# Pooling folds of one batch placed one to a half step, and VectorE's job number and first tile kept in two registers

## The chip, the cores and the metric

The kernel runs on one core of one Trainium2 chip. The metric is the device time of one execution in microseconds (us). Before the change it is 602.16 us, the median of three executions (602.12 to 604.27). The engines are called as the profile calls them: PE is TensorE's matmul, PEld its weight load, DVE is VectorE, ACT is ScalarE, POOL is GpSimd, SP is SyncE, which here only issues transfers.

## The reference, cut to what matters

Attention over pooled keys and values, followed by a mixture of eight experts in which each token goes to one expert:

```python
B, H, S, D = 8, 8, 576, 64                      # q, k, v: (8, 8, 576, 64)
k_p = k.reshape(B, H, 72, 8, D).mean(axis=3)    # every 8 rows of k and of v become one
v_p = v.reshape(B, H, 72, 8, D).mean(axis=3)
scores = q @ k_p.T / sqrt(D)
attn = softmax(scores)                          # over 72 keys
x = (attn @ v_p) -> rows of B*S = 4608 tokens, H*D = 512 wide
logits = x @ w_gate                             # 8 experts, 1024 hidden
e_idx = argmax(logits, axis=1)
out[mask_e] = gate_w * eom * (relu(x[mask_e] @ w1[e]) @ w2[e])
```

## The kernel before, in words

The 4608 tokens are 36 tiles of 128. The program has two parts.

**The attention part** goes through the tiles in half steps: tile i, heads 0 to 3 is half step i, tile i, heads 4 to 7 is half step i.5; there are 72. Each half step does three things for three different tiles, which makes a pipeline. It multiplies queries by pooled keys for its own tile (`scores`, PE, line 276, into one of three PSUM buffers `p_h`); DVE takes the maximum of each row (`peak`, line 282, tile name `m`), and ACT the exponentials (line 288). It transposes the probabilities of the tile two steps back (PE line 300, ACT line 301). And it multiplies those of the tile three steps back by the pooled values (`values`, PE line 310, into `p_y`, one PSUM buffer for each half of the heads); DVE then takes the reciprocals of the sums (line 327, `grec`) and writes the normalised rows out of PSUM (`normalise`, line 333, `xg`). Until line 333 of a half step is done, PE can't start `values` of the half step one whole step later, since both use the same `p_y` buffer.

The order of instructions on each engine is the order in which this loop calls them: every engine is a queue, and nothing is moved later. Work that belongs to no single tile is put between in two ways. `at(step, ...)` puts a call at the end of a certain half step: `at(s, ...)` runs at the end of half step s + 0.5. And `queue` holds generators, each a chain of small pieces of DVE work; `work(n)` (called three times in a half step, with 2, 1 and 1) takes up to n pieces of them. A generator that yields 0 may be taken again at once; one that yields 1 is passed over until the next half step.

The values of a batch b are first needed in the half step that I call f: f is 4.5, 9, 13.5, 18, 22.5, 27 and 31.5 for batches 1 to 7 (batch 0 has code of its own). Their eight rows per key lie side by side in one SBUF buffer, `rows`, loaded by one transfer (line 189). They are summed in three foldings. The first is POOL's (`halve_v`, line 224, five adds of about 0.7 us; three of them called at the end of half step f - 2.5, two at the end of f - 2). The other two are DVE's, for two parts of the buffer, which makes four adds, all of line 228, and called folds 1 to 4 here: fold 1 is `rows` 128x384, fold 2 `vp` 128x192, fold 3 `rows` 128x256, fold 4 `vp` 128x128. They come from the generator `pooled`. Fold 1 needs POOL's first three adds, fold 3 the last two. At the end of half step f PE transposes the folded values (`turn_v`, line 248, tile `vtr`), and ACT copies them for the gates' matmuls. The transfer of the next batch's values (line 189, on SP) goes into the same buffer and so waits for fold 4; the transfers of queries and keys behind it on SP's queue wait with it.

The other generators in `queue` are the routing (`route`): after each four tiles, some twenty pieces of DVE work decide to which expert each token goes, and POOL scatters the tokens' rows (line 441). `pooled` is put ahead of them.

**The expert part** runs the tokens through the experts in jobs of up to three tiles, with loops whose counts are read from a table that the routing made. PE's first layer is line 1031, the second line 1012. On DVE the function `body` (line 1210) is built once for each expert and each job size: it scales the last output of the job before (`last_output`, lines 1206 and 1204), subtracts high parts of the hidden layer (line 1215), splits weights (line 1192) and prepares the next job's inputs (`next_low`, line 1242; the wait is line 1163). Each wait compares a semaphore with a number made of `job` (the number of the job) and `u` (its first tile). Both are expressions: the sum of the counts of all experts before, plus the loop's own counter. At each use the sequencer works the whole sum out anew, in instructions that the trace calls FUSED_REGOPS and the order ISA.

Of the kernel before, what the change touches and what calls it, by code (L numbers as in the profile page):

```python
# [91 lines left out]
def attention_and_routing(ctx, tc, sh, qT, kT, v, wg, wst, xs):  # L92
    nc = tc.nc
# [132 lines left out]
    def pool_v(b, a, n):  # L226
        to = vt[:, part_v(a), 0:n] if n > D else pooled_rows(b)[:, part_v(a)]
        nc.vector.tensor_tensor(to, vt[:, part_v(a), 0:n], vt[:, part_v(a), n:2 * n], op=ALU.add)
# [293 lines left out]
    plan, queue = {}, []  # L522

    def at(step, f, *args):
        plan.setdefault(step, []).append((f, args))

    def pooled(b):
        for a in range(2):
            for n in (2 * D, D):
                pool_v(b, a, n)  # L530
                yield 0

    tick = [0]

# [14 lines left out]
    for b in range(1, B):  # L549
        f = S * b // P + 0.5 * (b % 2)  # L550
        at(f - 8.5, load_k, b)
        at(max(f - 5, 0), load_v, b)
        at(f - 4.5, load_q, b)
        for i, part in enumerate([(w, c, c + 1) for c in range(4) for w in (4, 2)] + [(1, 0, 4)]):
            step = f - 5.5 + 0.5 * (i // 2)
            at(step if step != -0.5 else 0, pool_k, b, nc.gpsimd, *part)
        at(max(f - 2.5, 1.5), scale_k, b)
        at(f - 3, halve_v, b, 0)
        at(f - 2.5, halve_v, b, 1)
        at(f - 2, lambda b: queue.insert(0, [pooled(b), 0, -1]), b)  # L560
        for c in range(3):
            at(f - 0.5 + 0.5 * c, place_v, b, c)
        at(f - 0.5, turn_v, b)
        at(f + 1.5, gate_v, b)
# [163 lines left out]
def experts(st, nc, sh, wst, xs, out):  # L728
# [49 lines left out]
    def mark(eng, hint, which):  # L778
        r, spot = which
        hint[spot] = eng.mark_branch_hint_location(hint[r])  # L780
# [64 lines left out]
    def started(e, size, rows, nth):  # L845
        return rows[E + 1] - 2 - nth if e == 0 and size == 3 else None
# [314 lines left out]
    def _(eng):  # L1161
        def xl(u, k):
            eng.wait_ge(q["xh"], u + k + 1)
            nc.vector.tensor_tensor(xt[:, 1, :, P * k:P * k + P], turned[k], xt[:, 0, :, P * k:P * k + P].bitcast(F32),
                                    op=ALU.subtract).then_inc(q["xl"], 1)
# [5 lines left out]
        def turns(job, read=None, more=None):  # L1171
            if read is not None:
                eng.wait_ge(q["xl"], read)
            eng.wait_ge(q["xd"], LANDED * (job + 1))
            turn(0)
            turn(1)
            if more is None or isinstance(more, int):
                if more:
                    eng.wait_ge(q["xl"], read + 1)
                turn(2)  # L1180
            else:
                with eng.If(more > 0):
                    eng.wait_ge(q["xl"], read + 1)
                    turn(2)
                with eng.Else():
                    turn(2)

        def split(some):
            for e, j in some:
                m, s, hi, lo = piece(e, j)  # L1190
                eng.wait_ge(q["wh"], 8 * e + j + 1 - EARLY)
                nc.vector.tensor_tensor(lo, s, hi.bitcast(F32), op=ALU.subtract).then_inc(q["wl"], 1)
# [10 lines left out]
        def output(k):  # L1203
            nc.vector.tensor_scalar(yb[k], p_y[k], sc[:, k:k + 1], None, op0=ALU.mult).then_inc(q["y"], 1)  # L1204

        def last_output(u):
            eng.wait_ge(q["l2"], u + 1)  # L1207
            output(2)

        def body(e, size, job, u, single, nth, more, last, late, hint):  # L1210
            n = size * P

            def low(f, src, n):
                eng.wait_ge(q["hh"], 8 * job + f + 1)
                nc.vector.scalar_tensor_tensor(ht[:, 1, f, 0:n], src, 0.0, ht[:, 0, f, 0:n].bitcast(F32),  # L1215
                                               op0=ALU.max, op1=ALU.subtract).then_inc(q["hl"], 1)

            def hidden(some, turned=False):
                for f in range(8):
                    low(f, p_h[f % DEEP][:, 0:n], n)  # L1220
                    split(some[f:f + 1])
                    if turned and f == 3:
                        turns(job + 1, u + 2, 3)
                eng.nop().then_inc(q["ad"], 8)

            def hidden_one(some):
                for f in range(9):
                    if f < 8:
                        eng.wait_ge(q["l1"], 8 * job + f + 1)
                        nc.vector.tensor_reduce(sums[:, f], p_h[f % DEEP][:, 0:2 * P].rearrange("p (x n) -> p n x", x=2),  # L1230
                                                axis=AX.X, op=ALU.add).then_inc(q["ad"], 1)
                    if f:
                        low(f - 1, sums[:, f - 1], P)
                        if f - 1 in POS:
                            split(some[POS.index(f - 1):][:1])

            with eng.If(job > 0):  # L1237
                last_output(u)
            done = started(e, size, rows, nth)

            def next_low():
                xl(u + size, 0)
                xl(u + size, 1)
                with eng.If(more > 0):
                    xl(u + size, 2)

            def begin_split(some):
                next_low()
                split(some[2:])

            if done is None:
                choose(eng, e, size, single, nth, hidden, hidden_one, split, done, late)
                next_low()
            else:
                choose(eng, e, size, single, nth, lambda some: (hidden(some), next_low()), None, begin_split, done, late,
                       lambda some: (hidden(some, True), next_low()))
            rest(eng, e, size, single, nth, split, 0, 99, done, late)
            finish(eng, e, size, single, last, split, 0, 4)
            if size == 3:
                mark(eng, hint, PAIRS)  # L1260
            elif e + 1 < E:
                mark(eng, hint, TRIPS)

            def close():
                turns(job + 2, u + size + 2, more)
                y(u, 0, job)
                if size == 3:
                    y(u, 1, job)

            if done is None:  # L1270
                close()
            else:
                with eng.If(done > 0):
                    y(u, 0, job, True)
                    y(u, 1, job, True)
                    with eng.If(counts(rows[0])[0] <= 1):
                        turns(job + 2, u + size + 2, more)
                with eng.Else():
                    close()
# [174 lines left out]
```

## Time and profile before

| | |
|---|---|
| median of three executions | 602.16 us |
| the profiled execution, its own time | 602.74 us |
| its span from first to last instruction | 600.8 us |
| TensorE's granted clock, mean share | 0.999 |
| PE busy | 572.1 us, 95% |
| PEld busy | 518.9 us, 86% |
| DVE busy | 363.7 us, 61% |
| ACT busy | 256.4 us, 43% |
| POOL busy | 223.9 us, 37% |

The 600.8 us are one execution; a busy time is the union of an engine's instructions. The attention part lies between about 9 and 154 us, the expert part between about 153 and 600 us. In nearly every fortieth of the span PE is busy for nine tenths or more, so what counts is where it is not, and on whom it waits there.

### The profile page before, as it was taken

To read this page: it belongs to the slowest core of one execution; us is meant where nothing else is said; L and a number is where in the kernel's file an instruction comes from. 1 tells how busy PE (TensorE), PEld (TensorE's weight loads), DVE (VectorE), ACT (ScalarE), POOL (GpSimd) and SP (SyncE) were. 2 spreads that over 40 slices of the span, in tenths; PEclk is the share of its full clock that TensorE was granted. 3 is DMA by queue.
4 is the path that set the end of the run, shared out by engine and by line. 5 is a ranking of instruction groups with operands and counts; after the bars stand their busy time and mean duration, and the time that the engine had idled before them with its cause. 6 is when DMAs were issued, how large, how long until landed. Compare 5 with 4: busy or idle time off the path is not lost.

```text
span 600.8 us, 11852 instructions
## 1 busy us (share of the span) xinstructions
PE 572.1 (95%) x3427; PEld 518.9 (86%) x3428; DVE 363.7 (61%) x892; ACT 256.4 (43%) x709; POOL 223.9 (37%) x331
## 2 busy tenths in 40 slices
PE   2899999999999999999999999999999999999996
PEld 2798898888888989898989898898998898989895
DVE  6788899988978725698575324664253832232323
ACT  2888988788525304266344121441140430202120
POOL 2849789851526322224224131232202422213131
PEclk9999999999999999999999999999999999999999
DMA  9767888975557433589656213363033112010111
GB/s 338 292 239 289 351 304 314 373 292 163 189 203 193 164 101 116 146 238 327 207 192 202 62 38 88 124 211 64 37 133 99 48 31 69 17 52 19 35 36 35
DMA packets 44683, 96.60 MB, mean 161 GB/s; under 512 B 5515, under 2 KB 28475, under 8 KB 41664
## 3 DMA queue, kind: packets, MB, share of 16 engines
q1 hardware_dynamic: 29328, 48.95, 25.4%
q10 hardware_dynamic: 7488, 27.27, 13.6%
q0 software_dynamic: 7792, 19.61, 9.2%
q14 instruction: 56, 0.46, 0.2%
q8 instruction: 19, 0.31, 0.2%
HBM read 76.36 MB, written 22.91 MB: 165 GB/s over the span
## 4 chain that ended last, share of the span: by engine, by line
PE 68%; issue 2%; DVEq 0%; DVE 0%; POOL 0%; POOLq 0%
PE p_h L1031 34%; PE p_y L1012 33%; PE p_y L665 1%; POOL out L1353 0%; DVE rows L1204 0%; DVEq L1207 0%; PE p_y L1068 0%; DVE q_even L1230 0%; DVEq L793 0%; POOLq L1318 0%; DVEq L767 0%; DVEq L1237 0%; DVEq L926 0%; DVEq L853 0%; DVEq L785 0%
## 5 line engine op out<-in xcount | busy, mean ns | idle before, releaser
L1113 ACT ACTIVATE ht<-p_h 128x384 fp32r<-128x384 f32 (+1 forms) x104 | 46.8, 450 | 246.4 <-PE p_h L1031 219.1
L1353 POOL DMA_INDIRECT out<-rows,dst x41 | 42.2, 1030 | 210.4 <-DVE rows L1204 207.3
L1031 PE MATMUL p_h<-xt,w1b 128*128 128x384 f32 (+1 forms) x736 | 115.5, 317 | 2.0 <-issue 2.0
L1031 PEld LDWEIGHTS p_h<-xt,w1b 128*128 128x128 f32 x736 | 114.4, 189 | 3.3 <-issue 2.9
L1215 DVE SCALAR_TENSOR_TENSOR ht<-p_h,ht 128x384 fp32r<-128x384 f32 (+1 forms) x104 | 52.3, 504 | 100.0 <-ACT ht L1113 90.6
L1012 PE MATMUL p_y<-w2b,ht 128*128 128x512 f32 x480 | 110.4, 390 | 0.0
L1012 PEld LDWEIGHTS p_y<-w2b,ht 128*128 128x128 f32 x480 | 89.8, 188 | 18.4
L1031 PEld LDWEIGHTS p_h<-xt,w1a 128*128 128x128 f32 x640 | 92.7, 190 | 2.6 <-DVE q_even L1230 1.2
L1031 PE MATMUL p_h<-xt,w1a 128*128 128x256 f32 (+1 forms) x640 | 93.7, 306 | 1.2 <-DVE q_even L1230 1.0
L1012 PE MATMUL p_y<-w2a,ht 128*128 128x512 f32 x408 | 94.0, 390 | 0.0
L1012 PEld LDWEIGHTS p_y<-w2a,ht 128*128 128x128 f32 x408 | 76.3, 188 | 15.6
L1204 DVE TENSOR_SCALAR rows<-p_y,sc 128x512 f32<-128x512 f32 x41 | 30.1, 742 | 84.3 <-PE p_y L1012 75.9
L288 ACT ACTIVATE p<-p_h,m 128x72 f32<-128x72 f32 x288 | 69.8, 347 | 16.3 <-DVE m L282 14.3
L310 PE MATMUL p_y<-vbd,pT 128*128 128x162 f32 (+3 forms) x400 | 68.7, 320 | 6.1 <-DVE xg L333 4.4
L1328 POOL DMA_INDIRECT rows<-xs,src x51 | 57.6, 1129 | 25.0 <-POOL src L1324 13.5
L310 PEld LDWEIGHTS p_y<-vbd,pT 128*128 128x128 f32 (+1 forms) x400 | 54.2, 179 | 11.1 <-issue 5.7
L441 POOL DMA_INDIRECT xs<-xg,where x36 | 36.0, 1000 | 38.4 <-DVE grec L327 17.2
L202 POOL TENSOR_TENSOR kq<-kq 128x288 f32<-128x288 f32 (+1 forms) x63 | 42.2, 675 | 17.4 <-DMA kq<-kT 14.4
L276 PE MATMUL p_h<-kbd,q_even 128*128 128x144 f32 (+1 forms) x160 | 28.7, 307 | 11.5 <-DMA q_even<-qT 8.8
L333 DVE TENSOR_TENSOR xg<-p_y,grec 128x240 f32<-128x240 f32 x72 | 35.2, 489 | 1.4
L276 PEld LDWEIGHTS p_h<-kbd,q_even 128*128 128x128 f32 (+1 forms) x160 | 22.8, 191 | 13.6 <-issue 9.5
L1168 DVE STREAM_TRANSPOSE turned<-rows 128x512 f32<-128x512 f32 x51 | 32.4, 686 | 3.2 <-DMA rows<-xs 1.5
(170 smaller groups left out, 657.7 us busy)
## 6 DMA issues: line engine op xcount, KB each, us to landing
stage<-wst ACTq DMA_DIRECT2D x52, 512.0 KB
rows<-v SPq DMA_DIRECT2D x8, 1280.0 KB
kq<-kT SPq DMA_DIRECT2D x7, 1152.0 KB
rows<-xs SPq DMA_DIRECT2D x36, 192.0 KB
stage<-wst SPq DMA_DIRECT2D x12, 512.0 KB, 5.0
kq<-qT SPq DMA_DIRECT2D x4, 1152.0 KB
q_even<-qT SPq DMA_DIRECT2D x3, 1152.0 KB, 8.5
rows<-xs SPq DMA_DIRECT2D x20, 128.0 KB
```

Of the source, the lines that this page charges most:

```text
L202: eng.tensor_tensor(k[:, :, 0:w], k[:, :, 0:w], k[:, :, w:2 * w], op=ALU.add)
L276: nc.tensor.matmul(s[r0:r0 + n, 144 * c:144 * c + 144], q_t[b][:, 2 * a + c, s0:s0 + n], kbd[b % 2][:, 2 * a + c, :], start=True, stop=True)
L288: nc.scalar.activation(pt[i % 3][:, o:o + KEYS], sv[:, h], AF.Exp, bias=m[:, h:h + 1])
L310: nc.tensor.matmul(av[r0:r0 + n, COLS * h:COLS * (h + n_heads)], pT[:, c, r0:r0 + n], vbd[b % 2][:, slot:slot + n_heads].rearrange("p h f ...
L333: nc.vector.tensor_tensor(xg[g][:, j, 0:LEAD + DM].rearrange("p (f h) -> p f h", h=H)[:, :, hs], avv[:, :, 0:GATE + D].rearrange("p h f -> ...
L441: ins = nc.gpsimd.indirect_dma_start(out=whole_rows(xs), out_offset=bass.IndirectOffsetOnAxis(ap=where, axis=0), in_=x.bitcast(I32), in_of ...
L1012: i = mm(to, ht[:, h, f, P * k:P * k + P], w[:, part, o:o + DM], start=(f == 0 and part == 0 and h == 0), stop=(f == 7 and h == 1))
L1031: i = mm(to, w[:, part, o:o + P], x, start=(d == 0 and k == 0), stop=(d == 3 and k == len(terms) - 1))
L1113: act(ht[:, 0, f, 0:size * P], p_h[f % DEEP][:, 0:size * P], AF.Relu).then_inc(q["hh"], 1)
L1215: nc.vector.scalar_tensor_tensor(ht[:, 1, f, 0:n], src, 0.0, ht[:, 0, f, 0:n].bitcast(F32), op0=ALU.max, op1=ALU.subtract).then_inc(q["hl" ...
L1328: nc.gpsimd.indirect_dma_start(out=xm[:, k].bitcast(I32), out_offset=None, in_=xs, in_offset=bass.IndirectOffsetOnAxis(ap=src[:, k:k + 1], ...
L1353: nc.gpsimd.indirect_dma_start(out=out, out_offset=bass.IndirectOffsetOnAxis(ap=dst[:, k:k + 1], axis=0), in_=yb[2 if k == size - 1 else k ...
```

## The change

The generator of the folds yields 1 and not 0, so that a half step takes one fold of a batch, and it is put into the queue half a step earlier. In DVE's part of the expert code two registers are set at the head of each job, and the rest of the job uses these.

```diff
@@ pooled(b)
             for n in (2 * D, D):
                 pool_v(b, a, n)
-                yield 0
+                yield 1
@@ for b in range(1, B)
-        at(f - 2, lambda b: queue.insert(0, [pooled(b), 0, -1]), b)
+        at(f - 2.5, lambda b: queue.insert(0, [pooled(b), 0, -1]), b)
@@ DVE's part of the experts
+        kept = [eng.alloc_register(name) for name in ("job_now", "u_now")]
+
         def body(e, size, job, u, single, nth, more, last, late, hint):
             n = size * P
+            for r, value in zip(kept, (job, u)):
+                eng.reg_mov(r, value)
+            job, u = (nc.s_assert_within(eng.snap(r), 0, most, skip_runtime_bounds_check_because="there are at most 50 slots")
+                      for r, most in zip(kept, (49, 49)))
```

The first place is DVE in half steps 3 to 4.5, where batch 1 is folded (f is 4.5). `m_0_` and `m_1_` are the maxima of two successive half steps, `grec` and `xg` the reciprocals and normalised rows of one half step, `vp_310` the folded values. Before:

```order
L282 TENSOR_REDUCE m_0_287<-p_h 128x4
L327 RECIPROCAL grec_293<-p_y 128x3
L333 TENSOR_TENSOR xg_291<-p_y,grec_293 128x80x3
L282 TENSOR_REDUCE m_1_307<-p_h 128x4
L228 TENSOR_TENSOR rows<-rows 128x3x128
L228 TENSOR_TENSOR vp_310<-rows 128x192
L327 RECIPROCAL grec_293<-p_y 128x5
L228 TENSOR_TENSOR rows<-rows 128x2x128
L333 TENSOR_TENSOR xg_291<-p_y,grec_293 128x80x5
L228 TENSOR_TENSOR vp_310<-rows 128x128
```

After, for the same half steps and two more:

```order
L282 TENSOR_REDUCE m_0_287<-p_h 128x4
L228 TENSOR_TENSOR rows<-rows 128x3x128
L327 RECIPROCAL grec_294<-p_y 128x3
L333 TENSOR_TENSOR xg_292<-p_y,grec_294 128x80x3
L282 TENSOR_REDUCE m_1_308<-p_h 128x4
L228 TENSOR_TENSOR vp_310<-rows 128x192
L327 RECIPROCAL grec_294<-p_y 128x5
L333 TENSOR_TENSOR xg_292<-p_y,grec_294 128x80x5
L282 TENSOR_REDUCE m_0_331<-p_h 128x4
L228 TENSOR_TENSOR rows<-rows 128x2x128
...
L282 TENSOR_REDUCE m_1_353<-p_h 128x4
L228 TENSOR_TENSOR vp_310<-rows 128x128
```

A reciprocal and a normalisation stand where rows are left out. Fold 1 has moved from half step 3.5 to 3, ahead of a normalisation; fold 2 stays in 3.5; fold 3 comes in 4 and fold 4 in 4.5, half a step and a whole step later than before. All batches move alike: folds 1 to 4 stand in half steps f - 1.5, f - 1, f - 0.5 and f, where all four stood in f - 1.

The second place is PE at the end of half step 4.5. Its order around the transposes of the folded values is the same before and after (names of buffers aside); this is after:

```order
L300 MATMUL ptr_1_348<-ident,p_75 128x128 x3
L310 MATMUL p_y<-vbd_69,pT_282 128x162
L310 MATMUL p_y<-vbd_69,pT_282 128x243
L310 MATMUL p_y<-vbd_69,pT_282 128x162
L248 MATMUL vtr_367<-ident,vp_310 128x128 x2
L248 MATMUL vtr_367<-ident,vp_310 64x128
L276 MATMUL p_h<-kbd_72,kq 128x144 x2
```

Nothing moved here: the transposes read what fold 4 writes, and fold 4 now stands in the same half step on DVE.

The third place is DVE at the head of a job in the code of a late expert. Before:

```order
L1237 ISA
L1237 COMPARE_AND_BRANCH
L1207 ISA x4
L1204 TENSOR_SCALAR rows<-p_y,sc 128x512
```

After:

```order
L1215 ISA x4
L1243 COMPARE_AND_BRANCH
L1207 REGISTER_ALU
L1204 TENSOR_SCALAR rows<-p_y,sc 128x512
```

The sums stand once ahead of the branch, and the wait is made from a register by one instruction. (Line numbers behind the change are six higher.) The same happens at `next_low` and at the end of the job. The routing's pieces shift by a few places between the folds, and with them POOL's scatters by one or two places; the instructions themselves are the same.

## Rows read from the trace of the kernel before

**Rows 1.** Stretches: us; busy PE, PEld, DVE, ACT, POOL; clock, DMA, GB/s.
```profile
20.00:154.00 134.00, 126.60 (x972) 113.52 (x973) 116.84 (x422) 113.44 (x448) 94.04 (x130) 1.00 0.78 289
200.00:596.00 396.00, 392.71 (x2177) 356.90 (x2176) 192.45 (x301) 114.24 (x200) 98.55 (x142) 1.00 0.35 104
```

**Rows 2.** Waits of PE: total us, times, longest us.
```profile
PE p_y L310 <- DVE xg L333: 4.4, 6, 1.5
PE p_h L1031 <- DVE q_even L1230: 1.0, 1, 1.0
```

**Rows 3.** Waits of DVE: the folds behind POOL's adds.
```profile
DVE rows L228 <- POOL rows L224: 4.4, 4, 1.6
```

**Rows 4.** Waits of SP's queue: the next batch's values.
```profile
SPq L189 <- DVE vp L228: 72.2, 6, 16.4
```

**Rows 5.** Timeline of DVE, batch 1: start us, us, instruction, [idle before].
```profile
23.83 1.07 DVE L228 TENSOR_TENSOR rows<-rows 128x384 f32<-128x384 f32 x1 [1.60 <-POOL rows L224]
...
26.52 0.61 DVE L228 TENSOR_TENSOR vp<-rows 128x128 f32<-128x128 f32 x1
27.05 0.45 DVE L282 TENSOR_REDUCE m<-p_h 128x4 f32<-128x288 f32 x1
27.42 0.16 DVE L327 RECIPROCAL grec<-p_y 128x3 f32<-128x3 f32 x1
27.62 0.41 DVE L333 TENSOR_TENSOR xg<-p_y,grec 128x240 f32<-128x240 f32 x1
27.94 0.45 DVE L282 TENSOR_REDUCE m<-p_h 128x4 f32<-128x288 f32 x1
...
28.52 0.58 DVE L333 TENSOR_TENSOR xg<-p_y,grec 128x400 f32<-128x400 f32 x1
```

**Rows 6.** Timeline of PE, batch 1.
```profile
23.81 0.72 PE L310 MATMUL p_y<-vbd,pT 128*128 128x162 f32 x4
...
26.75 1.20 PE L310 MATMUL p_y<-vbd,pT 128*128 128x162 f32 x6 [1.10 <-DVE xg L333]
27.79 0.49 PE L248 MATMUL vtr<-ident,vp 128*128 128x128 f32 x3
```

**Rows 7.** Timeline of POOL, batch 1.
```profile
21.71 3.78 POOL L224 TENSOR_TENSOR rows<-rows 128x256 f32<-128x256 f32 x5
...
26.19 5.32 POOL L202 TENSOR_TENSOR kq<-kq 128x288 f32<-128x288 f32 x8 [0.56 <-DMA kq<-kT]
```

**Rows 8.** Timeline of DVE, batch 2.
```profile
40.64 0.54 DVE L228 TENSOR_TENSOR rows<-rows 128x384 f32<-128x384 f32 x1
41.21 0.36 DVE L228 TENSOR_TENSOR vp<-rows 128x192 f32<-128x192 f32 x1
...
42.78 0.18 DVE L379 TENSOR_REDUCE gden<-ex 128x4 f32<-128x32 f32 x1
42.87 0.18 DVE L383 TENSOR_TENSOR pos<-rk,running 128x32 f32<-128x32 f32 x1
...
43.96 0.45 DVE L282 TENSOR_REDUCE m<-p_h 128x4 f32<-128x288 f32 x1
```

**Rows 9.** Timeline of PE, batch 2.
```profile
43.40 0.49 PE L248 MATMUL vtr<-ident,vp 128*128 128x128 f32 x3
```

**Rows 10.** Timeline of DVE, batch 3.
```profile
56.72 1.07 DVE L228 TENSOR_TENSOR rows<-rows 128x384 f32<-128x384 f32 x1 [1.07 <-POOL rows L224]
...
58.69 0.90 DVE L228 TENSOR_TENSOR rows<-rows 128x256 f32<-128x256 f32 x1
```

**Rows 11.** Timeline of PE, batches 3 and 5.
```profile
60.14 1.23 PE L310 MATMUL p_y<-vbd,pT 128*128 128x162 f32 x6 [1.49 <-DVE xg L333]
61.21 0.49 PE L248 MATMUL vtr<-ident,vp 128*128 128x128 f32 x3
...
93.94 1.20 PE L310 MATMUL p_y<-vbd,pT 128*128 128x162 f32 x6 [0.98 <-DVE xg L333]
```

**Rows 12.** The chain that ended last, in order of time: start us, us, what.
```profile
461.72 0.22 DVEq L1207
```

## The prediction

> **What bounds the kernel now.** I read the stretches first, then the waits of PE, then the timelines of the engines that PE waits for. Between 20 and 154 us, the attention part, PE is busy for 126.60 of 134.00 us, and DVE, ACT and POOL work beside it for 116.84, 113.44 and 94.04 us; in the expert part PE is busy for 392.71 of 396.00 us, DVE for 192.45 [rows 1]. So PE sets the end throughout. The change touches no instruction of PE; it can take away only what PE waits for DVE, and add to it. Two such waits count: in six places `values` waits for a normalisation, 4.4 us together, and once, in the expert part, PE waits 1.0 us for a reduction of DVE [rows 2]. If both went, the time would fall by 5.4 us. This is the most that the change can win.
>
> The timelines say where the 4.4 us come from. In batches 1, 3 and 5 DVE does the four folds in one half step, `xg` of that half step is late, and PE stands 1.10, 1.49 and 0.98 us [rows 6, 11]: 3.57 of the 4.4. But why is DVE late there? Fold 1 starts when POOL's third add ends: in batch 1 it had waited 1.60 us, in batch 3 1.07 [rows 5, 10], in four places together 4.4 us [rows 3]. It is POOL that holds up the odd batches, and the length of the folds comes on top.
>
> **The folds, batch by batch.** I take what a DVE instruction costs from start to start in batch 1: `m` 0.37 us (27.05 to 27.42), `grec` 0.20, a normalisation of three heads 0.32 [rows 5]; one of five heads lasts 0.58 where the other lasts 0.41, so I count 0.49. Folds beside an idle POOL: 0.54 and 0.36 for folds 1 and 2 [rows 8], and by size 0.36 and 0.24 for folds 3 and 4. Beside POOL's adds they took 1.07 (fold 1), 0.90 (fold 3) and 0.61 (fold 4) [rows 5, 10].
>
> Batch 1. POOL's five adds run from 21.71 us for 3.78 us [rows 7], and nothing in the change brings them forward, so fold 1 starts at 23.83 as before, only that DVE now stands in front of it with one normalisation and one `m` still undone. From there to the end of fold 4: fold 1, `grec`, `xg` 1.07 + 0.20 + 0.32; `m`, fold 2, `grec`, `xg` 0.37 + 0.36 + 0.20 + 0.49; `m`, fold 3, `grec`, `xg` 0.37 + 0.36 + 0.20 + 0.32; `m`, fold 4 0.37 + 0.24; together 4.87 us, so 28.7 us. The transposes of `vp` stand on PE at 27.79 [rows 6] and read what fold 4 writes: today it ends at 27.13 (26.52 + 0.61), then about 28.7. With folds 3 and 4 at their long durations it is 0.54 + 0.37 more, 29.6. PE thus comes to its next scores 1.0 to 1.9 us later than now. The first of its stalls is already inside this: `values` that started at 23.81 waits until the delayed `xg`, about 25.6, and the 1.10 us at 26.75 go. POOL adds keys from 26.19 us for 5.32 us [rows 7], beside all three later folds, so I take 1.5 us, nearer to the long durations.
>
> Batch 2 waits for no POOL today. Its `m` of half step 9 starts at 43.96, while the transposes start at 43.40 [rows 8, 9]: DVE is behind PE. If nothing in front of this `m` went, fold 4 would end at 43.96 + 0.37 + 0.24 = 44.57, 1.2 us late. But by the order seven small pieces of the routing, 0.09 us from start to start (42.78 to 42.87, rows 8), and fold 4 itself move behind it: 0.63 + 0.24 us less, so 43.7. I take 0.3 us.
>
> Batch 3 has the same sum from fold 1 at 56.72 [rows 10], with nine routing pieces between: 4.87 + 9 x 0.09 = 5.68, so 62.4 us, and 62.9 with the long fold 3, against transposes at 61.21 [rows 11]: 1.2 to 1.7 later. POOL's chain before these adds does not shift by all of what PE has lost by then, which gives some back: 1.2 us.
>
> Batches 4 to 7. Batch 5 is an odd one of the same kind with the smallest stall today (0.98); POOL's lead over the shifted PE has grown, and I take 0.4. Batch 4 I take like batch 2, 0.4. In batches 6 and 7 fold 1 need not wait, and DVE reaches the later half steps less behind, so the new wait and the small stalls that go about cancel: 0.1 and 0. Sum of the folds: 1.5 + 0.3 + 1.2 + 0.4 + 0.4 + 0.1 + 0 = 3.9 us.
>
> The ends of this term: below, the 4.4 us all go and no wait takes their place. Above, no batch gets anything earlier: 1.2 us (batch 2 undiminished) in seven batches, and in the three odd ones `grec`, `xg` and `m` (0.89 us) behind the fold as well: 8.4 + 2.7 = 11.1 us.
>
> Other sides of the move. SP's queue stands 72.2 us in six waits for fold 4 before it may load the next batch's values [rows 4]; fold 4 comes two half steps later, some 2 us, and the queries and keys behind it on that queue too. The next user, POOL, needs these values about three tiles later; I count nothing, and 2 us once if batch 2's came too late. Behind fold 1, which now waits longer in DVE's queue, stand one `grec` and `xg` (PE's `values` wait for it) and `m` (ACT's exponentials): that is in the sums. The waits between dependent folds (0.03 us after the end, as from 41.18 to 41.21, rows 8, where others overlap) go, but their gain is under 0.1 us each.
>
> A rule speaks against spreading the folds. The row: fold 1 took 0.54 us alone and 1.07 beside POOL's adds [rows 5, 8]. The Trainium skill (SBUF — State Buffer, section Who interferes with whom) says that a VectorE instruction with two inputs in SBUF contends with a GpSimd instruction that reads SBUF, and that whichever starts first holds the shared port for its whole length; the trace agrees with the doubling. By the short durations alone the sum of the folds would be 3.4 us, by this rule for every late fold it is the last rival below.
>
> **The registers.** In a late job the sequencer works out `u` in four pieces of about 0.22 us ahead of the last output [rows 12]. After the change it does the same pieces at the head of the job, then compares once; what is saved there is the piece that made `job`. At the later uses one register instruction replaces the sums, some 0.8 us a job, but DVE has 192.45 us of work in 396.00 [rows 1] and PE does not wait for it there. The price lies between -1.0 us (the one wait of PE that DVE causes goes) and +1.0 (it doubles, if the longer head comes at a bad place); I take -0.2.
>
> Sum: 3.9 - 0.2 = +3.7 us. The profiled execution took 602.74 us, which gives 606.4; it was 0.58 us above the median, 602.16, so 605.9 us for the median.
>
> **The rivals.**
> - The new waits and those that go cancel: 602.2 us. For it: PE has DVE behind it by only a little in the even batches, and DVE works off its backlog while PE stands. Against: the sums of batches 1 and 3 are 2.7 us by themselves.
> - The smoothing works: the six waits of 4.4 us go, 597.8 us. For it: DVE's four folds in one half step do make `xg` late. It needs POOL's adds to be done when DVE comes to fold 1 half a step earlier, and fold 4 to end before PE ends `values` of the same half step. Against: in three batches POOL is not even ready for today's place [rows 3], and today's `m` in batch 2 already starts behind the transposes.
> - The folds collide with POOL: folds 2, 3 and 4 in batches 1, 3 and 5 each take 0.5 us more (0.90 against 0.36 to 0.40): 9 x 0.5 = 4.5 on top, 610.4 us. It decides if POOL is at its adds in each of these half steps; with 94.04 of 134.00 us busy it is in most, but scatters are among them. The skill's rule on the shared port would give this.
>
> **How the numbers follow.** The forecast 0.52, with a range of its own from 603.2 to 609; cancelling 0.25; smoothing 0.13; collision 0.10. The measurement tells no change from one of about 0.5%, 3.0 us: below 599.2 is faster, above 605.2 slower. The forecast lies above 605.2 in some three of five cases (0.32), with the collision 0.42 for slower; the rest of the forecast and nearly all of cancelling make 0.43 for the same; smoothing and what is left 0.15 for faster. The range from 599.5 to 609.5 us holds the forecast and cancelling, and leaves out most of smoothing and half of the collision, under 0.2; the ends of the terms, 596.7 (-5.4) and 614.3 (+11.1 + 1.0), lie outside it as all of them would have to fall together.
>
> **What would show it.** Right: PE gets a new wait in its table, `vtr` (line 248) for `vp` (line 228), 3 to 6 us in four to seven places; DVE's wait for POOL's adds grows from 4.4 to 7 us or more; `values` of half step 4 waits in batch 1 in place of that of 4.5; the attention part ends some 4 us later and the expert part is as long as before within 0.5 us; fused register pieces at the wait of `next_low` are nearly gone. Wrong: no wait at `vtr` and no `xg` wait left (smoothing), or `vtr` waits that are matched by waits of `values` that vanished (cancelling), or an expert part that changes by over 1 us, which I hold for moved code and not for the registers.

## The result, and the profile after

| | before | after |
|---|---|---|
| first timing, median of 5 runs, us | 602.17 (602.12 to 604.27) | 610.24 (608.98 to 611.51) |
| ratio, 95% interval | | 1.0123 [1.0098, 1.0147] |
| second timing, ratio | | 1.0086 [1.0070, 1.0102] |
| profiled execution, us; its span | 602.74; 600.8 | 610.24; 608.5 |

The change makes the kernel slower, by 8.1 us in the first timing and 5.2 in the second; 3.7 were forecast, and the range ended at 609.5. The direction and the place of the new wait were right, the size was not. The ratios, here and below, leave out one execution in another state, 2016.15 us, of the kernel called "all four, later".

The waits of PE after, over the whole span: total us, times, longest. Below them the one row of before that is needed beside [rows 2].

```profile
PE vtr L248 <- DVE vp L228: 5.7, 5, 2.0
PE p_y L310 <- DVE xg L333: 1.9, 2, 1.1
PE p_y L665 <- PEq L1425: 1.8, 1, 1.8
PE p_h L1031 <- DVE q_even L1236: 1.0, 1, 1.0
PE p_y L665 <- issue: 0.6, 1, 0.6
```

```profile
PE p_y L665 <- PEq L1419: 1.0, 1, 1.0
```

Against [rows 2]: the six waits for `xg` fell from 4.4 to 1.9 us, and the transposes of `vp` now wait 5.7 us in five places for fold 4, which they did not do at all before; 3 to 6 us in four to seven places were forecast. The wait for `q_even`, the one that the registers could have touched, is 1.0 as it was. Two rows stand after the attention part, where the forecast had nothing: the entry into the expert blocks (line 665 released by the sequencer at line 1425, 1419 before), 1.8 us and 1.0 before, and a new wait of 0.6 us just ahead of it.

The wait of DVE for POOL's adds after, to set against 4.4 in four times [rows 3], and that of SP's queue for fold 4. Before, the seventh of these waits is put down to `rows` and not to `vp` (last line), so 72.2 [rows 4] and 8.8, 81.0 us in seven, stand against 91.8 in seven:

```profile
DVE rows L228 <- POOL rows L224: 5.0, 3, 2.6
```

```profile
SPq L189 <- DVE vp L228: 91.8, 7, 17.3
```

```profile
SPq L189 <- DVE rows L228: 8.8, 1, 8.8
```

The same stretches as in [rows 1]: us, busy PE, PEld, DVE, ACT, POOL, granted clock, DMA share, GB/s.

```profile
20.00:154.00 134.00, 124.57 (x959) 112.54 (x959) 111.92 (x406) 113.99 (x446) 89.44 (x125) 0.99 0.75 278
200.00:596.00 396.00, 393.26 (x2191) 359.08 (x2191) 197.68 (x308) 118.54 (x207) 102.21 (x144) 1.00 0.37 110
```

DVE and POOL are busy for less in the first stretch too, with fewer instructions, and ACT for 0.55 us more with two fewer. PE's clock reads 0.99. The stretches in which it fell, and the first of them in before:

```profile
80.00:83.75 3.75, 1.72 (x15) 1.45 (x14) 3.14 (x6) 2.91 (x13) 3.18 (x5) 1.00 0.50 172
83.75:87.20 3.45, 3.45 (x15) 3.30 (x14) 1.68 (x5) 2.20 (x8) 3.15 (x5) 0.51 0.97 332
180.00:182.70 2.70, 0.87 (x5) 0.59 (x4) 0.56 (x1) 0.00 (x0) 0.25 (x2) 1.00 0.00 0
182.70:186.20 3.50, 3.50 (x10) 2.71 (x9) 3.09 (x5) 2.00 (x2) 2.32 (x3) 0.51 0.89 313
```

```profile
83.75:87.20 3.45, 3.45 (x29) 3.12 (x29) 3.42 (x17) 3.45 (x16) 3.11 (x6) 1.00 1.00 415
```

Twice PE stood still, and in the 3.41 us behind it was granted 1.2 GHz in place of 2.4; the first time it did 15 matmuls, where the kernel before does 29 between the same two times. Half of 3.41 us is 1.7, and PE's lag behind before grows by 1.67 us in the first and 1.54 in the second. Before has none ahead of its last microseconds.

The first fall comes behind the worst of the new waits, in batch 4. DVE, POOL and PE there (start us, us, instruction, [idle before]):

```profile
79.47 0.42 DVE L228 TENSOR_TENSOR rows<-rows 128x256 f32<-128x256 f32 x1
...
80.51 0.45 DVE L282 TENSOR_REDUCE m<-p_h 128x4 f32<-128x288 f32 x1
80.87 1.50 DVE L228 TENSOR_TENSOR vp<-rows 128x128 f32<-128x128 f32 x1
```

```profile
80.43 0.96 POOL L441 DMA_INDIRECT xs<-xg,where  x1 [0.30 <-issue]
81.42 1.36 POOL L202 TENSOR_TENSOR kq<-kq 128x288 f32<-128x288 f32 x2
```

```profile
80.13 0.27 PE L248 MATMUL vtr<-ident,vp 128*128 128x128 f32 x1
82.43 0.44 PE L248 MATMUL vtr<-ident,vp 128*128 128x128 f32 x2 [2.03 <-DVE vp L228]
```

Fold 4, which I had put at 0.24 us, took 1.50 beside POOL's scatter and adds of keys, and all of it lies within PE's wait of 2.03. All folds of `vp` (2 and 4) after 20 us, after and before (min/median/max ns):

```profile
L228 DVE TENSOR_TENSOR vp<-rows x14: 281/349/1500, 25.9 to 135.7; 128x192 f32<-128x192 f32 x7, 128x128 f32<-128x128 f32 x7
```

```profile
L228 DVE TENSOR_TENSOR vp<-rows x14: 270/486/841, 24.9 to 128.0; 128x192 f32<-128x192 f32 x7, 128x128 f32<-128x128 f32 x7
```

The spread made the median shorter and the worst nearly twice as long.

### The profile page after: what moved, and what is told of

Its sections match the earlier page's. It is cut to its first block, busy times and chain, and to the rows that moved or that the text cites. A ratio compares the mean times of both kernels' runs of the same rounds, so it can differ in the third digit from the quotient of the medians.

```text
span 608.5 us, 11835 instructions
## 1 busy us (share of the span) xinstructions
PE 576.0 (95%) x3427; PEld 522.7 (86%) x3428; DVE 363.0 (60%) x892; ACT 258.7 (43%) x709; POOL 222.1 (37%) x331
## 4 chain that ended last, share of the span: by engine, by line
PE 67%; issue 2%; DVEq 0%; DVE 0%; POOL 0%; POOLq 0%
PE p_h L1031 33%; PE p_y L1012 32%; PE p_y L665 2%; DVEq L1215 0%; POOL out L1359 0%; DVE rows L1204 0%; PE p_y L1068 0%; DVE q_even L1236 0%; DVEq L793 0%; POOLq L1324 0%; DVEq L767 0%; DVEq L926 0%; DVEq L853 0%; DVEq L785 0%; DVEq L1235 0%
## 5 line engine op out<-in xcount | busy, mean ns | idle before, releaser
L276 PE MATMUL p_h<-kbd,q_even 128*128 128x144 f32 (+1 forms) x160 | 30.3, 320 | 11.7 <-DMA q_even<-qT 8.9
L282 DVE TENSOR_REDUCE m<-p_h 128x4 f32<-128x288 f32 x72 | 32.5, 451 | 7.6 <-PE p_h L276 5.0
L276 PEld LDWEIGHTS p_h<-kbd,q_even 128*128 128x128 f32 (+1 forms) x160 | 24.6, 203 | 13.3 <-issue 9.5
```

The costliest lines, as they stand in the source:

```text
L276: nc.tensor.matmul(s[r0:r0 + n, 144 * c:144 * c + 144], q_t[b][:, 2 * a + c, s0:s0 + n], kbd[b % 2][:, 2 * a + c, :], start=True, stop=True)
```

## The experiments

All ratios are to the kernel before, run on the same chip, with 95% intervals. "659 at" is the start of PE's first matmul of line 659, the end of the attention part; "entry" is PE's wait for line 1425 (1419 without the registers, and shifted by a line where a line was added). These two and the clock falls are read from one execution of each kernel.

| kernel | ratio | 659 at, us | entry, us | clock falls |
|---|---|---|---|---|
| before | 1 | 153.68 | 1.0 | none |
| registers alone | 0.9988 [0.9970, 1.0006] | 153.86 | 1.0 | none |
| folds alone | 1.0075 [1.0050, 1.0100] | 159.69 | 1.7 | 83.2 |
| after, again | 1.0086 [1.0070, 1.0102] | 157.00 | 1.9 | 181.0 |
| transposes later | 1.0051 [1.0037, 1.0066] | 155.95 | 1.7 | none |
| pairs | 1.0007 [0.9992, 1.0022] | 153.84 | 1.6 | none |
| pairs, later | 0.9996 [0.9980, 1.0012] | 153.70 | 1.8 | 177.7 |
| all four, later | 1.0017 [1.0004, 1.0031] | 153.78 | 1.6 | none |
| batches 1 to 3 later | 0.9953 [0.9937, 0.9970] | 152.45 | 1.0 | 245.5 |
| spread but for batch 7 | 1.0059 [1.0042, 1.0077] | 156.76 | 1.0 | none |
| batch 7 alone spread | 0.9988 [0.9977, 1.0000] | 153.24 | 1.0 | none |
| batches 1, 3, 5 later | 0.9960 [0.9947, 0.9974] | 152.77 | 1.0 | none |
| 1 to 3 later, 7 spread | 0.9936 [0.9916, 0.9957] | 151.16 | 1.0 | none |

**The two parts apart.** Registers alone, against the kernel before:

```diff
+        kept = [eng.alloc_register(name) for name in ("job_now", "u_now")]
...
+            for r, value in zip(kept, (job, u)):
+                eng.reg_mov(r, value)
+            job, u = (nc.s_assert_within(eng.snap(r), 0, most, skip_runtime_bounds_check_because="there are at most 50 slots")
+                      for r, most in zip(kept, (49, 49)))
```

> The kernel before, with the register part of the change alone; the folds stay all four in half step f - 1. My theory: the whole loss of 8.1 us comes from the folds, and the registers are worth nothing, since VectorE works 192 us of the 396 us of the expert part and TensorE does not wait for it there: 601.5 to 602.9 us, the wait of the scores at the block's entry about 1.0 us as before. Rival (moved code: the longer head of a job and other places of the instruction fetch cost in the change from attention to the expert part): 604 us or more, with the two stalls of TensorE at lines 665 and 659 longer than before.

Folds alone, against the kernel before:

```diff
-                yield 0
+                yield 1
-        at(f - 2, lambda b: queue.insert(0, [pooled(b), 0, -1]), b)
+        at(f - 2.5, lambda b: queue.insert(0, [pooled(b), 0, -1]), b)
```

> The kernel before, with the folds one to a half step, and the registers as before. My theory: all of the loss is here, 608.5 to 611 us, with TensorE's wait of the transposes of vp for fold 4 at 5 to 6.5 us and its wait of values for xg near 2 us. Rival (the registers' code carries some 3 us of the loss, in the change from attention to the expert part): 605 to 607.5 us.

And the changed kernel once more:

> The changed kernel again, beside the kernels of this call. In its first runs it stood at 1.0123 of the kernel before, while its two parts alone gave 1.0075 (folds) and 0.9988 (registers), which is 1.0063 together. My theory: the 2.5 us on top (a granted clock of half speed for 3.4 us before the expert part, and signals that came 2 us late there) fall in some runs and not in others, so the ratio here is 1.006 to 1.010. Rival: the two parts together cost more than their sum by way of moved code: 1.011 to 1.014 again.

The folds carry the loss. The registers' interval holds no change, -1.8 to +0.4 us. Their profile is 1.1 us shorter than that of before behind 200 us, in two steps of 0.5 and 0.6 us, but folds alone also shows the later one (0.6 us) and after, again, which has the registers, lacks the first, so neither is shown to be theirs. My rival that moved code costs 3 us is out. After, again lay in the range that the theory gave: it has one fall of the clock where the first profile has two.

**The transposes out of the way.** Against the changed kernel, as all diffs from here on:

```diff
-        at(f - 0.5, turn_v, b)
+        at(f, turn_v, b)
```

> The changed kernel with one thing more: the transposes of vp stand half a step later on TensorE (end of half step f + 0.5), so fold 4 has a half step's time before them. My theory (the loss is the wait of the transposes for fold 4, and what follows from it: the granted clock that falls after it, some 1.6 us each time, and the later start of the expert part): the wait goes from 5.7 us to under 1, xg waits stay near 2 us as against 4.4 before, and the time is 600 to 603.5 us, perhaps below the kernel before. Rival (the spread folds make every m and xg late, and the transposes only show it): the wait comes back at values and scores, 4 us or more, and the time stays over 607 us.

PE's waits between 20 and 200 us, and DVE's for POOL:

```profile
PE p_y L310 <- DVE xg L333: 2.6, 3, 1.2
PE p_y L665 <- PEq L1425: 1.7, 1, 1.7
PE p_y L310 <- DVE running L386: 1.3, 1, 1.3
PE vg L257 <- DVE pos L387: 1.1, 1, 1.1
```

```profile
DVE rows L228 <- POOL rows L224: 7.7, 4, 3.4
```

The transposes' wait went to 0.3 us, but the attention part ended 2.3 us late all the same, and the time was 1.0051 (607.0 us, where I had said 603.5 at most). My theory was half wrong: the waits came back under other names (pieces of the routing, which stand in DVE's queue with the folds), and DVE waits longer for POOL, 7.7 us as against 4.4 before and 5.0 in after; fold 1 stands half a step earlier than before, and POOL's adds did not move.

**POOL taken away.** GpSimd's adds are cut to a few columns, so that it is neither late nor beside the folds; the order on every engine stays.

```diff
-        eng.tensor_tensor(k[:, :, 0:w], k[:, :, 0:w], k[:, :, w:2 * w], op=ALU.add)
+        n = 4 if b else KEYS
+        eng.tensor_tensor(k[:, :, 0:w, 0:n], k[:, :, 0:w, 0:n], k[:, :, w:2 * w, 0:n], op=ALU.add)
...
-            nc.gpsimd.tensor_tensor(vt[:, c, 0:256], vt[:, c, 0:256], vt[:, c, 256:512], op=ALU.add)
+            nc.gpsimd.tensor_tensor(vt[:, c, 0:8], vt[:, c, 0:8], vt[:, c, 256:264], op=ALU.add)
```

> The changed kernel, with GpSimd's adds of keys and values of batches 1 to 7 cut to a few columns each (4 of the keys' columns, 8 of 256 of the values'), so the sums are left out and the routing comes out otherwise: only the attention part is read, up to TensorE's first matmul of line 659, which stands at 157.0 us in the changed kernel at full clock and at 153.7 in the kernel before. It is to be set against the next kernel. My theory (what the spread loses is GpSimd's: fold 1 half a step too early for its adds, and folds 3 and 4 beside its adds of keys): both go, the transposes' wait falls from 6.2 us to under 1.5, and the part ends within 0.6 us of the next kernel. Rival (the fourth fold stands behind VectorE's other work of half step f, and so after the transposes, GpSimd or not): the transposes still wait 3 us or more and the part ends 2 us or more after the next kernel's.

> The kernel before with the registers, and with the same cut of GpSimd's adds, sums left out; only the attention part is read. My theory: VectorE's wait for GpSimd's adds (3.4 to 4.4 us) goes to nothing and values' wait for xg from 4.4 us to 1.5 or less, so line 659 starts at 150 to 152 us as against 153.7. Rival (four folds in one half step make xg late by themselves): 153 us or more.

> The changed kernel with the adds of keys alone cut to 4 columns (those sums left out); the adds of values are whole. Only the attention part is read. My theory: fold 4 takes 0.28 us in every batch (0.76 to 1.50 beside adds of keys in the changed kernel), GpSimd comes earlier to the adds of values, the transposes' wait falls from 6.2 us to 2.5 or less, and line 659 starts at 153 to 155 us. Rival (only the order on VectorE counts): fold 4 is short, but the transposes wait 4 us or more, and 156 us or later.

The start of the first layer (line 660 here) in the three (before, with the registers and the cut; after with the cut; after with only the keys cut), and the transposes' waits in the last two:

```profile
147.82 4.44 PE L660 MATMUL p_h<-xt,w1a 128*128 128x384 f32 x24 [0.21 <-ACT xt L483]
```

```profile
148.80 4.46 PE L660 MATMUL p_h<-xt,w1a 128*128 128x384 f32 x24 [0.20 <-issue]
```

```profile
149.85 4.46 PE L660 MATMUL p_h<-xt,w1a 128*128 128x384 f32 x24 [0.20 <-issue]
```

```profile
PE vtr L249 <- DVE vp L229: 2.7, 3, 1.3
```

```profile
PE vtr L249 <- DVE vp L229: 1.9, 2, 1.4
```

Without POOL's adds the attention part of before is 5.9 us shorter, and its table of PE's waits has no row for `xg`: the 4.4 us were POOL's, and four folds in one half step cost PE no wait. The spread costs 1.0 us there (148.80 against 147.82) and 3.3 with POOL (157.00 against 153.68, both at full clock). So about two thirds of the loss hang on POOL; what is left goes with the order, by which the transposes still wait 2.7 us. The split is rough: each of these kernels ran once, and folds alone, with the same attention part as after, ended it 4.3 us late when its fall of the clock (1.7) is taken off. Neither my theory (within 0.6 us of each other, transposes under 1.5) nor its rival (2 us, transposes 3 or more) came out; and before with the cut and the kernel with the keys cut are earlier than I said (147.82, not 150 to 152; 149.85, not 153 to 155).

With the keys alone cut, all folds of `vp` take 0.28 to 0.39 us, and 7.1 of the 8.2 us that the full cut gives the changed kernel are there. So most of what POOL costs it hangs on the adds of keys: POOL comes later to the values by them, and late folds stand beside them. Before was not run with the keys alone cut, so their share in the loss against before is not shown.

**Folds at other places.** Pairs: two in half step f - 1, two in f - 0.5.

```diff
-                yield 1
+                yield 1 if n == D else 0
-        at(f - 2.5, lambda b: queue.insert(0, [pooled(b), 0, -1]), b)
+        at(f - 2, lambda b: queue.insert(0, [pooled(b), 0, -1]), b)
```

> The changed kernel with two folds in half step f - 1 (where the kernel before has all four) and two in f - 0.5, so the smoothing is half of the change's and needs nothing earlier from GpSimd. My theory: fold 4 ends before the transposes in most batches, their wait is 0 to 1.5 us, and the waits of values for xg fall from 4.4 to about 2.5 us: 600.5 to 603.5 us. Rival (whatever takes folds behind the next m makes the transposes wait): transposes wait 3 us or more and the time is over 605 us.

Pairs, later: the same, but

```diff
-        at(f - 2.5, lambda b: queue.insert(0, [pooled(b), 0, -1]), b)
+        at(f - 1.5, lambda b: queue.insert(0, [pooled(b), 0, -1]), b)
-        at(f - 0.5, turn_v, b)
+        at(f, turn_v, b)
```

All four, later: these two lines, and `yield 0`.

> The changed kernel with two folds in half step f - 0.5 and two in f, and the transposes of vp half a step later. Fold 1 is half a step later than in the kernel before, so GpSimd's adds have half a step more. My theory (most of the 4.4 us that values waits for xg in the kernel before comes from fold 1's wait for GpSimd, and only less of it from four folds in one half step): VectorE's wait for GpSimd goes under 1 us, the xg waits under 2 us, and the time is 0.994 to 0.999 of before. Rival (the waits are DVE's work in those half steps and come back elsewhere): 0.999 to 1.003.

> As the kernel with pairs later, but all four folds in half step f - 0.5: the kernel before with fold 1 half a step later, the transposes of vp half a step later, and the registers. My theory: nearly the same gain as with pairs, 0.995 to 1.000 of before, since it is GpSimd's lateness that counts and not the spreading. Rival (the length of four folds in one half step is what makes xg late): as before, 0.999 to 1.003, with xg waits still near 4 us.

Pairs came out as forecast in their waits (transposes 0.6 us, `xg` 2.3), without gain or loss in the attention part; the median, 603.68 us, lies just above what I gave, with before at 603.10 beside it. In the two later kernels DVE's wait for POOL is gone from the table, as forecast, and PE is 1.8 to 1.9 us ahead of before at half step 14.5; but from half step 20 (all four) or 24 (pairs) on it loses all of that, mostly at waits for the routing and for the later transposes (in the one with all four, `rk` waits 1.4 us for their copy). The rivals were right on the time; the waits for `xg` that one of them kept near 4 us fell to 1.4.

The changed kernel half a step later as a whole is not read: its fourth fold comes behind the load of the next batch's values in the order of the program, so it adds other numbers (1.1079 [1.1050, 1.1109]).

```diff
-        at(f - 2.5, lambda b: queue.insert(0, [pooled(b), 0, -1]), b)
+        at(f - 2, lambda b: queue.insert(0, [pooled(b), 0, -1]), b)
-            at(f - 0.5 + 0.5 * c, place_v, b, c)
-        at(f - 0.5, turn_v, b)
+            at(f + 0.5 * c, place_v, b, c)
+        at(f + 0.5, turn_v, b)
```

> The changed kernel with everything that it spreads half a step later: folds in half steps f - 1, f - 0.5, f and f + 0.5, the copies of vp half a step later, and the transposes of vp a whole step later. Fold 1 stands where the kernel before has it. My theory (with the transposes out of the way, what the spread still loses is fold 1 that waits for GpSimd's adds half a step early: 7.7 us of waiting in the kernel with the late transposes, 3.4 in the kernel before): VectorE's wait for GpSimd falls to 3 to 4.5 us and the time to 0.997 to 1.002 of before. Rival (late folds beside GpSimd's adds of keys, 1.4 to 1.5 us each for fold 4, cost as much wherever they stand): 1.004 or more, as with the late transposes. A loss of its own could come from the loads of the next values, which start one half step later still.

**Between the two parts of the kernel.** In the table the entry takes 1.0 us or 1.6 to 1.9, never anything between; in the cut kernels it is 1.0 in before and 1.5 in the two with the spread. The first `ht` of ACT, which waits for PE's first chunks of line 659, in before and after:

```profile
158.17 0.20 ACT L370 ACTIVATE ez<-zr 128x4 f32<-128x4 f32 x1 [0.95 <-DVE gden L379]
158.28 0.47 ACT L515 ACTIVATE ht<-p_h 128x384 fp32r<-128x384 f32 x1
```

```profile
163.13 0.21 ACT L370 ACTIVATE ez<-zr 128x4 f32<-128x4 f32 x1 [0.95 <-DVE gden L379]
165.28 0.49 ACT L515 ACTIVATE ht<-p_h 128x384 fp32r<-128x384 f32 x1 [1.95 <-remote]
```

The matmuls run at the same distances in both, yet after them ACT stands 1.95 us, released by something that the profile can't name ("remote"). In the trace's events PE's signals of two chunks and of `rk`, 3.75, 4.45 and 4.57 us after the first matmul of line 659 in before, come at 6.63, 6.69 and 6.76. `pos` (5.58 us in before, 7.65 in after), the job table and the entry are late in turn. I took this for the last batch's work. (Of the diffs from here on only the new lines are shown.)

```diff
+                yield 1 if b < 7 else 0
+        at(f - 2.5 if b < 7 else f - 2, lambda b: queue.insert(0, [pooled(b), 0, -1]), b)
```

> The changed kernel with the folds of batches 1 to 6 spread as it has them, and those of batch 7 as in the kernel before (all four in half step f - 1). My theory: what is lost ahead of the expert part (the signals of TensorE's first chunks of line 659 and of rk that come 0.6 to 2.7 us after those matmuls, then a longer entry into the blocks: 1.6 to 1.9 us as against 1.0) comes with the later pieces of the last batch, since it stood in all kernels that moved batch 7's folds and in none that left them (before, registers alone, batches 1 to 3 later): here the signals are on time (3.75, 4.45 and 4.57 us after the first of those matmuls), the entry takes 1.0 us, and the time is 1.005 to 1.008 of before. Rival (any move that makes the attention part end at another time or with other work left brings it): late signals again, entry 1.6 us or more, 1.008 or more.

Batch 7 alone has `b == 7` in both lines.

> The kernel before with the registers, and the folds of batch 7 alone spread as in the changed kernel. My theory: the attention part ends within 0.5 us of the kernel before, but the signals come late and the entry takes 1.6 us or more, so 0.8 to 2 us are lost: 1.000 to 1.003 of before. Rival: signals on time, entry 1.0 us, and with the registers' pieces 0.997 to 1.000.

With batch 7 as before:

```profile
PE vtr L248 <- DVE vp L228: 5.3, 5, 2.0
PE p_y L665 <- PEq L1425: 1.0, 1, 1.0
```

The signals are on time (3.75, 4.45 and 4.57 us) and the entry takes 1.0 us. The time is 1.0059 against 1.0086 of after, again; the intervals overlap a little, and their difference, 1.6 us, is near what this transition costs: by the end of the entry PE's lag grows by 0.6 to 1.9 us in the seven profiles that have it, without the fall of the clock that follows in three of them. But batch 7 alone does not bring it either, nor does the last kernel below, with batches 1 to 3 and 7 moved. It is there in all kernels of the table that move all seven batches and in none of the others; it belongs to the program and not to an execution (both profiles of after have it). Why PE's signals are held is not settled: its instructions there, their order and their distances are the same.

**A better version.** Late where the kernel before waits for POOL, as before elsewhere:

```diff
+        late = 0.5 if b < 4 else 0
+        at(f - 2 + late, lambda b: queue.insert(0, [pooled(b), 0, -1]), b)
+        at(f - 0.5 + late, turn_v, b)
```

(with `yield 0`).

> A try at a kernel better than both: registers; four folds in one half step as before, but for batches 1 to 3 half a step later (f - 0.5), with their transposes of vp half a step later; batches 4 to 7 as in the kernel before. In the kernel that did this in all batches TensorE was 1.9 us ahead of the kernel before by half step 14.5, and lost that again from half step 20 on. My theory: the 1.9 us stay, line 659 starts at 151.6 to 152.3 us, and the time is 0.995 to 0.999 of before, 1 us less of that if the signals of TensorE come late ahead of the expert part as they did in every kernel with moved folds so far. Rival (PE loses what it gains wherever routing's pieces come to stand next): line 659 at 153.3 or later, 0.999 to 1.003.

The same with `late = 0.5 if b in (1, 3, 5) else 0`:

> As the kernel that was faster (0.9953 of before: four folds half a step later for batches 1 to 3), but for batches 1, 3 and 5, the three where values waits for xg in the kernel before. My theory: 1.2 us more are won at half step 23, of which the later routing pieces take back some 0.6: line 659 starts at 151.6 to 152.3 us and the time is 0.993 to 0.997 of before. Rival (batch 5's later transposes meet the routing and lose all of it): 0.996 or more.

And batches 1 to 3 later with batch 7 spread, behind which no batch's keys are added:

```diff
+                yield 1 if b == 7 else 0
+        at(f - 2 + late - 0.5 * (b == 7), lambda b: queue.insert(0, [pooled(b), 0, -1]), b)
```

> The kernel that was faster (0.9953: four folds half a step later in batches 1 to 3), with batch 7's folds spread as in the changed kernel, which alone brought the attention part's end 0.4 us forward. My theory: the late signals of TensorE need batch 7 and an earlier batch moved together (neither alone brought them), so they come here: ScalarE waits some 1.7 us for its first ht, the entry takes 1.6 us or more, and the 0.7 us that batch 7 gives are lost: 0.995 to 0.998 of before. Rival (they need all seven batches moved, or hang on something else): signals on time, entry 1.0 us, line 659 at 151.6 to 152.1 us, 0.992 to 0.995.

PE's waits of the last, between 20 and 200 us:

```profile
PE vtr L248 <- DVE vp L228: 1.4, 1, 1.4
PE p_y L310 <- DVE xg L333: 1.2, 2, 1.0
PE p_y L666 <- PEq L1426: 1.0, 1, 1.0
```

All three beat both kernels, if only by 0.4 to 0.6% of before, the last with 0.9936 [0.9916, 0.9957], 599.16 us. In it my theory on the late signals was wrong and the rival right. Batch 5 moved later gave 1.2 us and lost as much to the routing, as its rival said.

## Why the prediction was wrong

- **What bounds the kernel**: right for the attention part. PE sets the end, and what it waits for DVE is what moves there.
- **The sum of the folds, +3.9 us**: measured 3.3 us at full clock (157.00 - 153.68, after, again; 4.3 in folds alone without its fall), so this sum was near, but partly by luck, as errors cancel. In after, again, PE's lag behind before, read at the starts of its scores a half step or two after each batch's fold 4, grows by 1.36 us in batch 1 (forecast 1.5), 0.27 in 2 (0.3), 0.85 in 3 (1.2), 2.38 in 4 (0.4), -0.49 in 5 (0.4), 0.40 in 6 (0.1) and -1.45 in 7 (0). Batch 4 was the mis-sized term: I took it "like batch 2" and counted fold 4 at 0.24 us; it took 1.50 beside POOL, and fold 1 came before POOL's adds were done (DVE waits 0.71 us for them in this batch, where before it did not wait). The total of that wait, of which I said 7 us or more, came to 5.0, with the longest, 2.6, in batch 1.
- **"An expert part that is as long as before within 0.5 us"**: this is the step that failed. Between the attention part and 205 us 3.2 us were lost in the first profile (PE is 8.16 us behind against 4.96): 1.9 with the late signals and the longer entry, 1.5 in the fall of the clock behind it, less 0.2. Behind that 0.5 came back. I had looked only at the instructions that the change moves, and priced a stall at its length; neither this transition nor a fall of the clock is in any of the rows that I read. My own reading of such a change, moved code, is out as well: registers alone moves that code and loses nothing.
- **The clock**: a term that I put at nothing without a reason; two falls in the first profile, 3.2 us, one in the second, 1.6. The whole span is then 3.3 + 1.7 (clock at 83.75) + 1.9 (late signals and entry) + 1.5 (clock at 182.7) - 0.7 = 7.7, as measured (608.5 - 600.8). This holds for the profiled execution. Two of the five of the first timing had a granted clock of 1.000 throughout and still took 608.98 and 609.22 us, where the sum without the falls gives 606.7 (602.17 + 4.5); they have no trace, and these 2 us stay unexplained. In the second timing the one with 1.000 took 606.72, where it gives 607.3 (602.76 + 4.5).
- **The registers, -0.2**: nothing that can be told from zero, as forecast, and the wait for `q_even` is unchanged. The fused register pieces at the wait of `next_low` (line 1163) went from 47 to none, as forecast, and DVE's pieces in all from 182 (26.5 us) to 131 (19.2). The head of a job did not get shorter: near the end it holds five pieces of line 1215, 0.15 to 0.21 us each, where before has four of line 1207 [rows 12].
- **SP's queue**: 10.8 us more of waiting, 1.5 in each of seven waits where I took some 2. POOL then waits 2.2 us once for batch 2's values, the 2 us that I named and left out of the sum; no fold of that batch waits for POOL behind it.
- **The rivals**: collision had the right cause for the largest term, batch 4, and a chance of 0.10 only; it looked for it in batches 1, 3 and 5. The trace had the two durations of fold 1, 0.54 and 1.07 [rows 5, 8]; I used the pair for the odd batches and not for the even ones. The rule of the Trainium skill (SBUF — State Buffer, section Who interferes with whom) spoke for it, and the cut adds agree: with the keys' adds cut no fold of `vp` takes over 0.39 us. Its other half, that the one that starts first holds the port, the profile's starts don't bear out: fold 4 of batch 4 starts at 80.87, POOL's add at 81.42, and fold 4 takes 1.50 us; but spans on POOL are rough.

"Smoothing" was worth nothing even where POOL is taken away, since four folds in one half step cost PE no wait there.

## What to carry to other kernels

Before spreading an engine's work, ask what the late work waits for: here one producer was late, and moving its consumer later for three batches won 0.5%, and spreading it in all seven lost 0.9 to 1.2%. When work moves, price it at the duration that it has beside its new neighbours on other engines, batch by batch, and not at its best one. A stall of the tensor engine may cost more than its length: look at the granted clock behind it.

## What was not expected of the hardware

- A granted clock of 1.2 GHz, half of the full 2.4, for 3.41 us behind PE's stalls of 2.03 us (batch 4; in folds alone too, behind 2.04) and of 1.8 to 1.9 us at the entry in three profiles; behind entries of 1.6 and 1.7 us in four others it did not fall, nor at the entry in the seven with 1.0. In batches 1 to 3 later it fell behind 1.85 us of waiting at 242.7 to 244.6 us. In after, again, and in the kernel spread but for batch 7 the wait of 2.0 us in batch 4 came without a fall, so the length of the stall alone does not tell.
- A fold beside a scatter of POOL alone is nearly as short as by itself (fold 4: 0.27 to 0.39 us, against 0.27 to 0.28 in before with POOL idle); with POOL's adds beside it fold 4 took up to 1.51 us (after, again) and fold 2 up to 1.94 (pairs, batch 7).
- Signals of PE that arrive up to 2.9 us later than in another kernel with the same matmuls (6.63 against 3.75), as told above.
